# When the block sums run, and where a batch's last PSUM bank is copied, in a gated attention followed by a two-matrix feed-forward layer

## The chip, the cores and the metric

The kernel runs on one core of a Trainium2 chip. The core has a matrix engine (TensorE, PE in the profile), a vector engine (VectorE, DVE), a scalar engine (ScalarE, ACT), a general engine (GpSimd, POOL) and a queue that only issues transfers (SyncE, SP). Each runs its own instructions in the order in which they are written and waits for the others by semaphores. TensorE writes its results into PSUM, which is kept here as two pairs of banks and four single banks; everything else lies in SBUF. The metric is the device time of one execution in microseconds (us), the median of several runs.

## The reference, cut to what matters

```python
# u, v: (8, 3008, 256); z: (8, 3008, 64); w_in: (256, 2048); w_out: (2048, 256)
scores = (1 / S) * z @ z.transpose(0, 2, 1)          # S = 3008
attn   = maximum(scores, 0) ** 2
x      = (u * (attn @ v)).reshape(8 * 3008, 256)
h      = x @ w_in
out    = (h / (1 + exp(-1.702 * h))) @ w_out
```

## The kernel before

Each of the 8 batches is cut into 6 chunks of 512 tokens (the last is shorter). For a chunk, the scores against blocks of keys go into a pair of PSUM banks (`sc`), ACT applies Relu (`rl`), DVE squares it (`a`), and TensorE multiplies by V into two single banks (`o`); DVE multiplies those by u (`gate`, tile `xt`). The scores are symmetric, so many blocks are not computed again but transposed by transfers on the SP queue (`tt`, `ad`). `attend` (L324) gives a chunk as a list of steps; in the main loop (L792) a step n of chunk i comes after what is written out for it: transposes of u, loads, and `take` (L757), which issues the scores, the Relu and the square of one or two units ahead of their use. The table `SCHED` (L725) says at which steps `take` is called; for the first chunk of batches 1 to 6 that is once each at n = 5, 9, 13 and 17, twice at 24, and every third step from 30 on.

The feed-forward layer works on pairs of chunks, s = 0, 1, 2 (chunks 0 and 1, 2 and 3, 4 and 5). `up_group(b, q)` (L407) makes one of 48 groups of a batch, 16 for each pair: four matmuls into a bank pair (`hg`, two such pairs in all, shared with the scores), the gelu on ACT into one of two buffers `gf` (L435), and a scaling into half precision, `gt`, on DVE (L441), or on ACT for q % 8 in 1, 3, 5 from q = 16 on (L439). So a group's matmuls need the gelu of two groups before to be done, and a group's gelu needs the scaling of two groups before.

The second matrix product of a pair is done in seven products instead of eight, a scheme of Strassen's kind: the operands are block sums `S1` to `S4` of the `gt` tiles (`pair_sum`, L547, on DVE) and sums of the weights. A pair needs 16 sums. They are appended to a list `SUMS` when their `gt` tiles are written, and `some_sums(most)` (L458) issues one of them, or two where the list is longer than `most`. The products P1 to P7 (`pair_product`, L574) accumulate in three single banks; a finished bank is copied by ACT (L607, L609) or added by DVE (L611) into the output tile `y`, which is transposed and stored (`store`).

The first 16 groups of a batch, the head (q below `LAGY` = 16), run inside the attention steps of chunk 4 (of chunk 5 in the last batch). There are no products yet. The other groups follow after chunk 5, one group and one half product in turn (loop at L840). The products left over at the end run alone (L856), the drain; then `take(b + 1, 2)` issues the next batch's first two units, and what is left in the list `AFTER` is issued (L867). In batches 0 to 6 that is one instruction, the copy of the bank that P4 of the last pair leaves (L607). The order of all engines is the order of the program text; nothing is reordered.

Of the kernel before, what the change touches and what calls it, by code (L numbers as in the profile page):

```python
# [15 lines left out]
def kernel(  # L16
# [13 lines left out]
    AF = mybir.ActivationFunctionType  # L30
# [23 lines left out]
    FSC = csc * csc * float(S) * float(S)  # L54

    dve, act, pe, sp, pool = nc.vector, nc.scalar, nc.tensor, nc.sync, nc.gpsimd
# [263 lines left out]
    def full(b):  # L320

        return NCH - 2 if b < B - 1 else NCH - 1
# [74 lines left out]
    def blocks(b):  # L397

        return [(i, CH if i < NCH - 1 or b % 2 else LFULL) for i in range(NCH)]

    def paired(b, s):

        return b < B - 1 or s < NCH // 2 - 1
# [3 lines left out]
    def up_group(b, q):  # L407
        s, r = divmod(q, 2 * NFG)
        pair = paired(b, s)
        if pair:  # L410
            fg, e = (TILES if q >= 2 * NFG or b else TILES0)[r // 2], r % 2
            if fg >= NFG // 2:
                e = 1 - e
            k = 2 * s + e
        else:
            k, fg = divmod(q, NFG)
        i, n = blocks(b)[k]
        hg = ps2.tile([P, FFG, CH], F32, name="hg", tag="ps2")
        for e in range(FFG):
            ff = fg * FFG + e  # L420
            for c in range(NCC):
                pe.matmul(  # L422
                    hg[:, e, :n], W1[:, c, ff * P:(ff + 1) * P], XT[b, i][:, c, :n],
                    start=(c == 0), stop=(c == NCC - 1),
                )
        if pair:
            if r % 2 == 0:
                GT[b, s, fg, "pair"] = pa.tile([P, FFG, 2, CH], F16, name="gt", tag="tt", bufs=14)
            g = GT[b, s, fg, "pair"][:, :, k % 2, :n]
        else:  # L430
            if fg % 2 == 0:
                GT[b, k, fg // 2] = pa.tile([P, CB, CH], F16, name="gt", tag="tt", bufs=14)
            g = GT[b, k, fg // 2][:, (fg % 2) * FFG:(fg % 2 + 1) * FFG, :n]
        gf = pw.tile([P, FFG, CH], F32, name="gf", tag="gf")
        act.activation(gf[:, :, :n], hg[:, :, :n], AF.Gelu_apprx_sigmoid, scale=1.0 / FSC)  # L435
        if pair and q not in (LAGY - 7, LAGY - 6):
            some_sums()
        if q >= LAGY and q % 8 in (1, 3, 5):
            act.activation(g, gf[:, :, :n], AF.Copy, scale=FSC)  # L439
        else:  # L440
            dve.tensor_scalar(g, gf[:, :, :n], FSC, None, ALU.mult)  # L441
        if not pair:
            some_sums(8)
        if pair:
            some = (("S1", "S2", "S3"), ("S4",))[r % 2] if fg >= NFG // 2 else ()
            SUMS.extend([lambda m=m, fg=fg: pair_sum(b, s, fg - NFG // 2, m) for m in some])
            if r == 2 * NFG - 2 and s == NCH // 2 - 1:
                some_sums()
        elif fg in (NFG - 3, NFG - 1):
            SUMS.extend(left_sums(b, k, fg == NFG - 1))  # L450
# [7 lines left out]
    def some_sums(most=3):  # L458
        for s_ in [SUMS.pop(0) for _ in range(min(len(SUMS), 1 + (len(SUMS) > most)))]:
            s_()  # L460
# [37 lines left out]
    def left_sums(b, k, last):  # L498

        some = [("S1", 0), ("S2", 0)]  # L500
        if last:
            some = [("S1", 1), ("S2", 1)] + [(name, h) for name in ("S3", "S4") for h in range(2)]
        return [lambda m=m: left_sum(b, k, *m) for m in some]
# [70 lines left out]
    def pair_product(b, s, name, half):  # L574
        if name == "odd":
            odd_block(b, s)
            return
        w = blocks(b)[2 * s + 1][1]
        right = {
            "P1": W2K[:, LO, 0], "P2": W2K[:, HI, 0], "P3": W2K[:, HI, 1], "P4": WT[:, 3],  # L580
            "P5": WT[:, 0], "P6": WT[:, 1], "P7": WT[:, 2],
        }[name]
        raw = {"P1": "a11", "P2": "a12", "P4": "a22"}
        form = {"P3": "S4", "P5": "S1", "P6": "S2", "P7": "S3"}
        new = name in ("P1", "P2", "P5")
        if new and half == 0:
            ST[b, s, "bank" + name] = ps1.tile([P, CH], F32, name="st", tag="ps1")
        bank = ST[b, s, "bank" + {"P6": "P1", "P7": "P1", "P4": "P1", "P3": "P5"}.get(name, name)][:, :w]
        for ff in range(half * NFF // 4, (half + 1) * NFF // 4):
            m, f = divmod(ff, FFG)  # L590
            while name in form and (b, s, form[name], m) not in ST:
                SUMS.pop(0)()
            lhs = pair_part(b, s, raw[name])(m) if name in raw else ST[b, s, form[name], m]
            pe.matmul(  # L594
                bank, right[:, ff], lhs[:, f], start=new and ff == 0, stop=ff == NFF // 2 - 1, skip_group_check=True,
            )
        if half == 0:
            return
        for e, at in ((0, "P1"), (1, "P5")):
            if name == at:  # L600
                Y[b, 2 * s + e] = pw.tile([P, NCC, CH], F32, name="y", tag="y")
        copy = {"P1": (0, 0), "P5": (1, 1), "P6": (0, 1), "P4": (1, 0)}
        outs = {"P3": (0, 1), "P7": (1, 1), "P2": (0, 0)}
        e, c = copy.get(name) or outs[name]
        y = Y[b, 2 * s + e][:, c, :w]
        if name == "P4" and s == NCH // 2 - 1:
            AFTER.append([0, lambda: act.activation(y, bank, AF.Copy, scale=1.0 / FSC)])  # L607
        elif name in copy:
            act.activation(y, bank, AF.Copy, scale=1.0 / FSC)  # L609
        else:  # L610
            dve.scalar_tensor_tensor(y, bank, 1.0 / FSC, y, ALU.mult, ALU.add)  # L611
        last = s == NCH // 2 - 1
        if name == "P4" and last:
            LAST2.extend([lambda: store(b, 2 * s), lambda: store(b, 2 * s + 1)])
        elif name == "P2" and not last:
            store(b, 2 * s)
        elif name == "P4":
            AFTER.append([2, lambda: store(b, 2 * s + 1)])

    AFTER = []  # L620

    def product(b, k, name):
        mm = pairs(b, k)
# [87 lines left out]
    LAGY = 2 * NFG  # L711
# [49 lines left out]
    def fill(b):  # L761
        assert not queue
        queue.extend(u_ for i in range(NCH) for u_ in pieces(b, i))
# [28 lines left out]
    for b in range(B):  # L792
# [5 lines left out]
        for i in range(NCH):  # L798
            host = b + 1 if more and i == NCH - 1 else b
            if host > b:  # L800
                fill(host)
                LATE.append(host)
            for n, step in enumerate(attend(b, i, b == 0 and i == 0)):
                if b == 0 and i == 0 and n in (5, 24):
                    load_u(0, n // 24)
                if b == 0 and i == 0 and n == 2:
                    copies = first_zt(3)
                if b == 0 and i == 0 and n == 3:
                    copies()
                if b == 0 and i == 0 and n in FIRST_CAST:  # L810
                    first_cast(FIRST_CAST[n], True)
                if b == 0 and i == 0 and n in FIRST_ZT:
                    first_zt(FIRST_ZT[n])()
                if (i, n) in turn:
                    turn_u(b, turn[i, n])
                if (i, n) in ((3, 3), (3, 26) if more else (4, 14)) and LAST2:
                    LAST2.pop(0)()
                if (i, n) in load:
                    load_u(b, load[i, n])
                if b == 0 and (i, n) in CASTW:  # L820
                    cast_w(CASTW[i, n])
                if b == 0 and (i, n) in LOADW:
                    load_w(LOADW[i, n])
                if more and (i, n) == (NCH - 2, 2 if b else 16):
                    load_z(b + 1)
                if b == 0 and i == NCH - 1 and n in (8, 30, 42):
                    wsums.pop(0)()
                take(host, sched[i].get(n, 0))
                if i == full(b) and n >= HEAD and (n - HEAD) * LAGY // (2 * NJ - 10) >= head and head < LAGY:
                    up_group(b, head)  # L830
                    head += 1
                step()
# [7 lines left out]
        for q in range(head, nup):  # L840
# [7 lines left out]
            prods.pop(0)()  # L848
            for a_ in AFTER:
                a_[0] -= 1  # L850
            while AFTER and AFTER[0][0] < 0:
                AFTER.pop(0)[1]()
            if q >= 44 and late:
# [9 lines left out]
        if more:  # L863
            while late:
                late.pop(0)[1]()
            take(b + 1, 2)
            while AFTER:  # L867
                AFTER.pop(0)[1]()


# [28 lines left out]
```

## Time and profile before

| | |
|---|---|
| median of 3 runs | 1182.12 us (1180.68 to 1183.69) |
| profiled execution, its own time | 1179.04 us |
| its span, first to last instruction | 1177.2 us, granted TensorE clock 0.999 |
| PE busy | 1169.1 us, 99% |
| DVE busy | 870.7 us, 74% |
| ACT busy | 837.3 us, 71% |
| POOL busy | 212.4 us, 18% |
| copies at L607 | 7, of 0.50 or 0.60 us |

A row of the timeline gives the start in us from the span's start, the duration, the engine, the line of the kernel, the operation, the tiles (out<-in) with their shapes, and the number of like instructions that are merged in it; in brackets stands how long the engine was idle before it and what ended that. A row of the waits gives who waited for whom: us in total, how often, the longest. [...]

### The profile page before, as it was taken

To read this page: it belongs to the slowest core of one execution; us is meant where nothing else is said; L and a number is where in the kernel's file an instruction comes from. 1 tells how busy PE (TensorE), PEld (TensorE's weight loads), DVE (VectorE), ACT (ScalarE), POOL (GpSimd) and SP (SyncE) were. 2 spreads that over 40 slices of the span, in tenths; PEclk is the share of its full clock that TensorE was granted. 3 is DMA by queue.
4 is the path that set the end of the run, shared out by engine and by line. 5 is a ranking of instruction groups with operands and counts; after the bars stand their busy time and mean duration, and the time that the engine had idled before them with its cause. 6 is when DMAs were issued, how large, how long until landed. Compare 5 with 4: busy or idle time off the path is not lost.

```text
span 1177.2 us, 20867 instructions
## 1 busy us (share of the span) xinstructions
PE 1169.1 (99%) x7996; PEld 575.3 (49%) x7996; DVE 870.7 (74%) x1386; ACT 837.3 (71%) x941; POOL 212.4 (18%) x294
## 2 busy tenths in 40 slices
PE   9999999999999999999999999999999999999998
PEld 3544455444454445544455445554445544554446
DVE  7789866878658786587865877668876698664876
ACT  7878864688646886478864787647876478672785
POOL 3033101232012320132101321014200241001000
PEclk9999999999999999999999999999999999999999
DMA  9998399854998559975499755996559975697023
GB/s 224 207 130 124 73 171 163 98 94 85 174 154 101 91 99 175 154 94 87 99 171 151 102 89 110 173 158 91 90 98 176 142 108 83 115 172 140 1 36 72
DMA packets 459027, 143.47 MB, mean 122 GB/s; under 512 B 424624, under 2 KB 453040, under 8 KB 458928
## 3 DMA queue, kind: packets, MB, share of 16 engines
q1 hardware_dynamic: 402464, 102.36, 53.6%
q0 software_dynamic: 55104, 38.49, 22.1%
q8 instruction: 62, 1.02, 0.4%
q10 hardware_dynamic: 1360, 1.31, 0.4%
q14 instruction: 37, 0.30, 0.1%
HBM read 60.29 MB, written 24.64 MB: 72 GB/s over the span
## 4 chain that ended last, share of the span: by engine, by line
PE 96%; ACT 2%; DVE 1%; issue 0%; ACTq 0%; DVEq 0%
PE o L367 39%; PE hg L422 27%; PE st L594 23%; PE sc L235 6%; PE st L642 1%; ACT rl L256 1%; PE yp L568 1%; ACT gf L435 0%; DVE gt L441 0%; PE w L99 0%; DVE s L560 0%; ACT y L607 0%; ACT ZT L143 0%; DVE ut L202 0%; DVE s L558 0%
## 5 line engine op out<-in xcount | busy, mean ns | idle before, releaser
L435 ACT ACTIVATE gf<-hg 128x1024 f32<-128x1024 f32 (+1 forms) x384 | 383.1, 1001 | 124.0 <-PE hg L422 102.2
L256 ACT ACTIVATE rl<-sc 128x1024 f16<-128x1024 f32 (+1 forms) x301 | 288.2, 993 | 167.4 <-PE sc L235 123.2
L422 PE MATMUL hg<-xt,W 128*128 128x512 f16 (+1 forms) x1408 | 353.4, 374 | 1.6 <-ACT gf L435 1.6
L367 PEld LDWEIGHTS <-V 64*128 64x128 f16 (+1 forms) x4098 | 239.2, 94 | 231.3 <-issue 9.5
L367 PE MATMUL o<-a,V 64*128 64x512 f16 (+3 forms) x2278 | 298.1, 368 | 0.4 <-DVE a L270 0.4
L441 DVE TENSOR_SCALAR gt<-gf 128x1024 f16<-128x1024 f32 (+1 forms) x288 | 204.8, 712 | 107.3 <-ACT gf L435 105.0
L270 DVE TENSOR_TENSOR a<-rl 128x1024 f16<-128x1024 f16 (+1 forms) x266 | 178.1, 674 | 116.3 <-ACT rl L256 114.2
L195 POOL DMA_DIRECT2D uq<-in_u_dram x168 | 115.0, 694 | 727.3 <-PE sc L235 469.8
L422 PEld LDWEIGHTS <-W 128*128 128x128 f16 x1536 | 149.5, 98 | 178.8 <-issue 6.0
L367 PE MATMUL o<-tt,V 64*128 64x512 f16 (+1 forms) x1518 | 234.0, 377 | 0.0
L235 PE MATMUL sc<-ZT 64*128 64x512 f16 (+3 forms) x688 | 118.1, 356 | 0.9 <-ACT ZT L143 0.3
L594 PEld LDWEIGHTS <-WT 128*128 128x128 f16 x736 | 72.0, 98 | 79.7 <-issue 0.8
L439 ACT ACTIVATE gt<-gf 128x1024 f16<-128x1024 f32 (+1 forms) x96 | 98.1, 1021 | 3.1
L594 PE MATMUL st<-gt,W 128*128 128x512 f16 (+1 forms) x368 | 89.9, 370 | 0.0
L594 PE MATMUL st<-s,WT 128*128 128x512 f16 (+1 forms) x368 | 89.2, 370 | 0.0
L594 PE MATMUL st<-gt,WT 128*128 128x512 f16 (+1 forms) x368 | 88.7, 370 | 0.0
L594 PEld LDWEIGHTS <-W 128*128 128x128 f16 x552 | 53.8, 98 | 58.2
L384 DVE TENSOR_TENSOR xt<-o,ut 128x512 f16<-128x512 f32 x80 | 51.4, 684 | 27.9 <-PE o L367 27.9
L558 DVE TENSOR_TENSOR s<-s,gt 128x1024 f16<-128x1024 f16 (+1 forms) x92 | 62.3, 677 | 1.0
L556 DVE TENSOR_TENSOR s<-gt 128x1024 f16<-128x1024 f16 (+1 forms) x92 | 60.9, 662 | 2.1
L560 DVE TENSOR_TENSOR s<-gt,s 128x1024 f16<-128x1024 f16 (+1 forms) x92 | 60.9, 662 | 0.0
L235 PEld LDWEIGHTS <-ZT 64*128 64x128 f16 x688 | 39.7, 94 | 43.3 <-issue 8.6
(66 smaller groups left out, 686.3 us busy)
## 6 DMA issues: line engine op xcount, KB each, us to landing
out_dram<-yo SPq DMA_DIRECT2D x156, 128.0 KB, 2.8
uq<-in_u_dram POOLq DMA_DIRECT2D x140, 128.0 KB, 3.5
V<-in_v_dram POOLq DMA_DIRECT2D x35, 256.0 KB, 6.6
tt<-a SPq DMA_TRANSPOSE x232, 3.4
uq<-in_u_dram POOLq DMA_DIRECT2D x28, 112.0 KB, 5.0
out_dram<-yo SPq DMA_DIRECT2D x28, 96.0 KB, 6.6
uq<-in_u_dram SPq DMA_DIRECT2D x20, 128.0 KB, 4.1
wst<-in_moe_w_in_dram POOLq DMA_DIRECT2D x4, 512.0 KB, 5.9
```

Of the source, the lines that this page charges most:

```text
L195: eng.dma_start(uq[k * QW:(k + 1) * QW, :n // QW].rearrange("t q c k -> t q (c k)"), src[:, :, cs])
L235: pe.matmul(sc[:, r, :q1 - q0], zt[h, 2 * kp + r, :], zt[h].rearrange("d n p -> d (n p)")[:, q0:q1], start=True, stop=True,)
L256: act.activation(rl[:, :, :n], sc[:, :, :n], AF.Relu, scale=csc)
L270: dve.tensor_tensor(a[:, :, :n], rl[:, :, :n], rl[:, :, :n], ALU.mult)
L367: ins = pe.matmul(acc[c][:, :n], V16[b][h, j].rearrange("p (c k) -> p k c", k=NCC)[:, c], weights(b, i, j)[h], start=(k, m) == first[c], s ...
L422: pe.matmul(hg[:, e, :n], W1[:, c, ff * P:(ff + 1) * P], XT[b, i][:, c, :n], start=(c == 0), stop=(c == NCC - 1),)
L435: act.activation(gf[:, :, :n], hg[:, :, :n], AF.Gelu_apprx_sigmoid, scale=1.0 / FSC)
L439: act.activation(g, gf[:, :, :n], AF.Copy, scale=FSC)
L441: dve.tensor_scalar(g, gf[:, :, :n], FSC, None, ALU.mult)
L556: dve.tensor_tensor(s_, a21, a22, ALU.add)
L558: dve.tensor_tensor(s_, ST[b, s, "S1", m], a11, ALU.subtract)
L594: pe.matmul(bank, right[:, ff], lhs[:, f], start=new and ff == 0, stop=ff == NFF // 2 - 1, skip_group_check=True,)
```

## The change

There are two parts.

In a head (q < 16) `some_sums` is no longer called between a group's gelu and its scaling. It is called behind the scaling, in those groups where q % 4 is 0, 1 or 2, with the limit 8 instead of 3, so that it issues one sum a time. From q = 16 on, and in groups that are not paired, the order is as it was.

The copy of the last pair's P4 bank goes into a list of its own, `COPY`, and is issued in the next batch's first chunk ahead of step 22, instead of behind the drain's `take`. The loop that emptied `AFTER` at the end of a batch is gone.

```diff
@@ up_group
         act.activation(gf[:, :, :n], hg[:, :, :n], AF.Gelu_apprx_sigmoid, scale=1.0 / FSC)
-        if pair and q not in (LAGY - 7, LAGY - 6):
+        if pair and q >= LAGY:
             some_sums()
         if q >= LAGY and q % 8 in (1, 3, 5):
             act.activation(g, gf[:, :, :n], AF.Copy, scale=FSC)
         else:
             dve.tensor_scalar(g, gf[:, :, :n], FSC, None, ALU.mult)
-        if not pair:
+        if not pair or q < LAGY and q % 4 < 3:
             some_sums(8)
@@ pair_product
         if name == "P4" and s == NCH // 2 - 1:
-            AFTER.append([0, lambda: act.activation(y, bank, AF.Copy, scale=1.0 / FSC)])
+            COPY.append(lambda: act.activation(y, bank, AF.Copy, scale=1.0 / FSC))
...
-    AFTER = []
+    AFTER, COPY = [], []
@@ main loop
                 if (i, n) in ((3, 3), (3, 26) if more else (4, 14)) and LAST2:
                     LAST2.pop(0)()
+                if (i, n) == (0, 22) and COPY:
+                    COPY.pop(0)()
...
             take(b + 1, 2)
-            while AFTER:
-                AFTER.pop(0)[1]()
```

## The prediction

> **What bounds the kernel now.** I read the page's busy shares first, then TensorE's own waits, then the timeline around every place where a matmul starts late.
>
> ```profile
> PE 1169.1 (99%) x7996; PEld 575.3 (49%) x7996; DVE 870.7 (74%) x1386; ACT 837.3 (71%) x941; POOL 212.4 (18%) x294
> ```
> ```profile
> PE hg L422 <- ACT gf L435: 1.6, 2, 1.1
> ```
>
> TensorE is busy for 99% of the span; only stalls of TensorE are to be won. The list of waits understates them: four matmuls in a row last 1.03 us and each is recorded 0.38 long, so they start (1.03 - 0.38)/3 = 0.216 apart, and a matmul that starts up to 0.16 late leaves no idle row. So I compare starts. From the head of the first batch (q numbers the up groups of a batch):
>
> ```profile
> 78.46 0.59 PE L367 MATMUL o<-tt,V 128*128 128x512 f16 x2
> 79.52 1.02 PE L422 MATMUL hg<-xt,W 128*128 128x512 f16 x4 [0.47 <-ACT gf L435]
> 81.28 0.65 DVE L551 TENSOR_TENSOR gt<-gt 128x1024 f16<-128x1024 f16 x1
> 81.85 0.68 DVE L560 TENSOR_TENSOR s<-gt,s 128x1024 f16<-128x1024 f16 x1
> 82.44 1.31 DVE L441 TENSOR_SCALAR gt<-gf 128x1024 f16<-128x1024 f32 x1
> 83.85 1.02 ACT L435 ACTIVATE gf<-hg 128x1024 f32<-128x1024 f32 x1 [2.24 <-DVE gt L441]
> 84.93 1.02 PE L422 MATMUL hg<-xt,W 128*128 128x512 f16 x4 [1.14 <-ACT gf L435]
> ```
>
> Here two sums (81.28, 81.85) stand ahead of the scaling of q11 (82.44), its end frees gf for the gelu of q13 (83.85), and that frees the PSUM pair for the matmuls of q15 (84.93). Two attention matmuls before it started at 83.19 and 83.41, so q15 was due at 83.62: 1.31 late. Likewise q12 was due at 78.46 + 0.43 = 78.89 and came at 79.52 (0.63), and q11 was 0.14 late at 77.60. Sum 2.08 us. In later batches only q15 is late. Its due time is the start of q14 plus six matmuls, 1.30: 228.12 against 228.28, 374.39/374.50, 663.94/664.04, 953.35/953.46, and nothing in the batches at 517 and 807: 0.5 in all.
>
> The other place is a batch's first chunk:
>
> ```profile
> 308.42 0.60 ACT L607 ACTIVATE y<-st 128x512 f32<-128x512 f32 x1
> 308.90 1.04 ACT L256 ACTIVATE rl<-sc 128x1024 f16<-128x1024 f32 x1
> 310.00 0.39 PE L235 MATMUL sc<-ZT 64*128 64x512 f16 x2
> ```
>
> The last bank's copy (308.42) stands ahead of the Relu of step 5 (308.90 to 309.94), which frees the score pair that step 13 writes. Step 9's scores began at 308.77; with their 0.11 and four row-tile pairs at 0.216, step 13 was due at 309.74: 0.26 late. In batches of the other parity (163.72, copy 0.50) it is 0.15. Seven starts, 4 x 0.15 + 3 x 0.25 = 1.35.
>
> **The change, part by part.** *The copy (L606, L867, loop at L816).* It moves on ACT's queue alone, from behind the two drain Relus to step 22 of the next first chunk; no DMA and nothing on SP, POOL or DVE moves with it. With it gone, step 5's Relu starts at 308.42 and ends at 309.46; step 13 is due at 309.74, so its stall goes whole: -1.35. Next late would be step 17, which needs step 9's Relu (about 309.97 against 310.82): free. In its new place the copy takes 0.60 (0.50) of this row's idle:
>
> ```profile
> 313.20 6.39 ACT L256 ACTIVATE rl<-sc 128x896 f16<-128x896 f32 x7 [0.68 <-PE sc L235]
> ```
>
> Step 17's Relu ends at 312.53, the copy ends about 313.05, and the next Relu starts at 313.20: cost 0, by 0.15. That cover matters: the seven Relus behind it run back to back at 0.91 against scores every 0.865, and the last scores (318.79) follow the Relu that frees them (318.68) by 0.11. A copy later by d would cost up to 7 x (d - 0.25). The store of that block is issued in chunk 3, from about 344 on, over 30 us later. The bank is held some 4 us longer. Four banks serve these tiles; the other two product banks are emptied by 305.23 (three evacuations of 157.58 to 159.37 in the other parity) and chunk 0's first attention matmul starts at 306.61, so two free banks are there: 0. The upper bound, a chunk 0 that waited for the held bank, would be 306.6 to 312.5, 5.9 per batch; but those matmuls come before the Relus that the copy is queued behind, so the program could not run at all, and I exclude it.
>
> [...]
>
> *The sums in the head (L436, L442).* Same instructions, other order. Before, 13 of the 16 sums of the first pair ran in q0 to q15: two each at q11 and q12, none at q9 and q10, always ahead of the scaling. After, 9 run (8 in batch 0), one behind each scaling where q % 4 < 3. A sum occupies DVE for 0.60 (81.85 to 82.44 is 0.59), a scaling 0.60 (85.00 to 85.60). A pair is 1.20 and the groups come every 1.29 or 1.51, so DVE keeps up, and each fourth group has no sum.
>
> I walk batch 0 through by these rows, keeping POOL's copies where they are (0.6 added to whatever DVE runs, as in the 1.31 of 82.44). The scaling of q7 ends at 75.5 instead of 76.43, so q9's gelu starts at 75.7 and q11 is on time. q10's scaling, a sum and the 1.17 transpose (step 28) follow to 80.6; q11's scaling ends at 81.3 instead of 83.75, q13's gelu runs 81.35 to 82.37, and q15 is due at 82.85. The 2.08 goes whole, with 0.5 to spare. In batch 1, q11's scaling ends at 226.45 instead of 227.11, q13's gelu ends at 227.6 and q15 is due at 228.12; batches 2, 4 and 6 are alike: -0.5.
>
> *What comes back at q16.* Instead of 3 sums, 7 (8 in batch 0) are left, and from q16 on they run in twos ahead of the scalings as before. There DVE comes straight from the last gates:
>
> ```profile
> 102.18 0.68 DVE L558 TENSOR_TENSOR s<-s,gt 128x1024 f16<-128x1024 f16 x1
> 102.78 0.94 DVE L441 TENSOR_SCALAR gt<-gf 128x1024 f16<-128x1024 f32 x1
> ...
> 103.81 1.02 ACT L435 ACTIVATE gf<-hg 128x1024 f32<-128x1024 f32 x1 [0.88 <-DVE gt L441]
> ...
> 104.88 1.02 PE L422 MATMUL hg<-xt,W 128*128 128x512 f16 x4
> ```
>
> In batch 0 (above) the gelu of q18 ends at 104.83 and q20 starts at 104.88, on time, with nothing left. DVE cannot bring its lead from the head: at 98.64 it waits for a Relu (ended 98.59) and from there has 3.5 us of fixed work. One more sum ahead of q16's scaling makes q20 late by 0.6 less the 0.05: +0.55. Then 5 sums more than now run by q20, so q20's scaling comes at about 110.9 instead of 108.27, which is 110.3 on the delayed TensorE; q22's gelu starts at 111.0 instead of 110.63 and q24 is late by 0.37 less its slack of 0.1: +0.28. Together +0.83. Bounds: 0 if DVE gains its lead after all, 3.0 (five sums at 0.60) if nothing is hidden; I take 0.83 since it follows the rows next to it.
>
> In batches 1 to 6 the same gelu leaves room:
>
> ```profile
> 391.64 0.68 DVE L441 TENSOR_SCALAR gt<-gf 128x1024 f16<-128x1024 f32 x1
> ...
> 392.42 1.02 ACT L435 ACTIVATE gf<-hg 128x1024 f32<-128x1024 f32 x1
> ...
> 394.45 1.03 PE L422 MATMUL hg<-xt,W 128*128 128x512 f16 x4
> ```
>
> It ends at 393.44, 1.01 ahead of q20 (1.04 in batches 1, 3, 5); ACT's copy of q17 holds it to 392.42 anyway. Late by 0.5 it still hides. ACT is full there and carries that 0.5 on for some groups, under margins of 1.0 to 1.3. The products need the sums in time: the second half of P5 wants its S1 at about 395.75 and gets it at 394.2. In batch 7 q18's gelu waits for ACT. Cost 0.
>
> **The sum.** -1.35 - 2.08 - 0.5 + 0.83 = -3.1 us. The profiled execution took 1179.04 (span 1177.2 and 1.8 around it), so it would become 1175.9. It is 3.1 below the median of the runs; taken from that, 1182.12 - 3.1 = 1179.0.
>
> **Rivals.** *No payback*: batch 0's tail absorbs the sums; -3.93, 1178.2. For it: DVE sheds five sums (3.0) before q16. Against it: the 0.05 margin. *The order saves nothing in the head*: DVE is just as full, a sum behind one scaling delays the next, and q15 stays late; then only the copy counts, with the payback: -0.5, 1181.6. Against it: 4 to 5 sums fewer. For it: POOL's copies (81.94 to 83.21) slow whatever DVE runs. *Slower*: the backlog at q16 outruns the margin of 1.01 to 1.04 in all batches. It decides when the gelu of q18 is late by more than 1.03: each further 0.1 costs 0.7 over seven batches, so at 2.1 late (three and a half sums instead of the one counted) 7 x 1.07 eats the 3.93 and adds 3.5: 1185.7; at four sums, 2.4 late, 7 x 1.37 - 3.9 gives 1187.8. For it: the 0.94 scaling beside POOL's V loads. Against it: half the margin is left by my count.
>
> **How the numbers follow.** Likeliest 0.42, no payback 0.28, head saves nothing 0.15, slower 0.15. What a measurement can tell is about 0.3%, 3.5 us; the runs shown spread over 3.0. Faster by that means below 1178.6: I give it 0.45 of the likeliest and 0.75 of the no-payback case, 0.40. Slower (above 1185.7) has its case's 0.15, same the rest, 0.45. The range goes from no payback less half the runs' spread, 1176.5, past the third case to 1184.0, leaving out the slower case and little below.
>
> **What would show it.** In the changed profile: step 13's scores of each first chunk 0.97 after step 9's; an ACT copy in the gap before the run of seven Relus, which still starts 0.40 behind its scores; hg starts of the batch 0 head at 1.3 or 1.5 without the 0.63 and 1.31; DVE with sums behind scalings. The payback shows as q20 and q24 of batch 0 late. Wrong would be: hg q20 late in batches 1 to 6, an idle TensorE at 313 to 319, or an attention matmul waiting for a PSUM bank.

## The result, and the profile after

The changed kernel takes 1178.19 us (median; 1175.54 to 1181.57). The kernel before, run beside it on the same chip, took 1180.22 (1178.61 to 1183.69). The ratio is 0.9981 with a 95% interval of 0.9972 to 0.9990, so the change takes off 2.2 us, between 1.2 and 3.3. That is less than the 0.3% that the prediction named as the bound for telling a time from no change, though the interval excludes no change. The sum of -3.1 lies inside this interval, near its edge; the absolute 1179.0 was reckoned from a median of 1182.12, which the later runs of the kernel before put 1.9 lower.

The profiled execution took 1177.70 us (span 1175.9), against 1179.04 (1177.2). First the busy times and TensorE's longest waits, from the page and from the list of waits of the changed kernel:

```profile
PE 1167.6 (99%) x7996; PEld 552.7 (47%) x7996; DVE 874.3 (74%) x1386; ACT 837.8 (71%) x941; POOL 209.6 (18%) x294
```
```profile
PE hg L422 <- ACT rl L256: 1.7, 1, 1.7
PE w L99 <- DVE nil L75: 1.2, 1, 1.2
```

The wait for a gelu that headed this list before (1.6 in two places) is gone. In its place stands one wait of 1.7 that nobody forecast. As in the prediction, I count from starts: what every matmul's start comes later than its predecessor's streaming time (0.216 for one of 512 columns), summed over the execution, was some 13.0 us before and is 11.8 now, a difference like that of the spans.

**The copy's place.** The timeline of the changed kernel in the first chunk of batch 2:

```profile
308.81 0.27 PE L235 MATMUL sc<-ZT 64*128 64x256 f16 x2
309.79 0.38 PE L235 MATMUL sc<-ZT 64*128 64x512 f16 x2
312.21 0.59 ACT L607 ACTIVATE y<-st 128x512 f32<-128x512 f32 x1
312.59 0.54 PE L235 MATMUL sc<-ZT 64*128 64x448 f16 x4
312.99 6.39 ACT L256 ACTIVATE rl<-sc 128x896 f16<-128x896 f32 x7 [0.19 <-PE sc L235]
```

Step 13's scores (309.79) come 0.98 behind step 9's (308.81), where they came 0.26 late before. The copy (312.21 to 312.80) lies in the gap ahead of the run of seven Relus, which still starts 0.40 behind its scores. All seven stalls of 0.15 and 0.25 are gone, and no attention matmul and no product waits for one of the four single PSUM banks (the wait of 1.7 above is for a score pair in batch 0, and has another cause).

**The head of batch 0.** TensorE of the changed kernel at q13, q14 and q15:

```profile
81.72 1.03 PE L422 MATMUL hg<-xt,W 128*128 128x512 f16 x4
82.58 0.81 PE L367 MATMUL o<-tt,V 128*128 128x512 f16 x3
83.23 1.03 PE L422 MATMUL hg<-xt,W 128*128 128x512 f16 x4
84.09 0.59 PE L367 MATMUL o<-tt,V 128*128 128x512 f16 x2
84.53 1.03 PE L422 MATMUL hg<-xt,W 128*128 128x512 f16 x4
```

The groups come 1.51 and 1.30 apart, which is their streaming time. The three stalls of 0.14, 0.63 and 1.31 are gone.

**What took their place.** Three things. The first is a late load, on VectorE and TensorE:

```profile
60.99 1.25 DVE L202 STREAM_TRANSPOSE ut<-uq 128x1024 f32<-128x1024 f32 x1 [3.15 <-DMA uq<-in_u_dram]
...
63.81 1.02 PE L422 MATMUL hg<-xt,W 128*128 128x512 f16 x4 [1.72 <-ACT rl L256]
```

The transpose of u for chunk 3 waited 3.15 for its load and held up the squares queued behind it; the first up group came 1.89 late. In the profile before, the same transpose ran at 57.98 without a wait. This code is untouched by the change, and it runs ahead of everything that the change moves. The second is the first weight sum (L488, issued at step 8 of chunk 5 of batch 0), which now waits for the load of w_out:

```profile
91.57 1.23 DVE L488 TENSOR_TENSOR WT<-W 128x1024 f16<-128x1024 f16 x1 [1.24 <-DMA W<-in_moe_w_out_dram]
```

Before, it started at 91.47 straight behind VectorE's preceding work, with its second quarter of w_out landed at 90.95, only half a microsecond to spare. In the profile of before:

```profile
91.47 1.22 DVE L488 TENSOR_TENSOR WT<-W 128x1024 f16<-128x1024 f16 x1
```

The third is the payback behind q16, in other places than forecast:

```profile
102.56 1.02 ACT L435 ACTIVATE gf<-hg 128x1024 f32<-128x1024 f32 x1
...
103.45 0.69 DVE L441 TENSOR_SCALAR gt<-gf 128x1024 f16<-128x1024 f32 x1
...
105.25 0.68 DVE L556 TENSOR_TENSOR s<-gt 128x1024 f16<-128x1024 f16 x1
...
105.34 1.24 PE L594 MATMUL st<-s,WT 128*128 128x512 f16 x4
...
106.58 0.68 DVE L441 TENSOR_SCALAR gt<-gf 128x1024 f16<-128x1024 f32 x1
...
107.36 1.02 ACT L435 ACTIVATE gf<-hg 128x1024 f32<-128x1024 f32 x1 [1.02 <-DVE gt L441]
...
108.44 1.02 PE L422 MATMUL hg<-xt,W 128*128 128x512 f16 x4
```

P5's four matmuls at 105.34 last 1.24 instead of 1.03: its second half waits for S1 (105.25 to 105.93), 0.22. The matmuls of q22 (108.44) come 0.29 late, behind q20's gelu (107.36), which waited for q18's scaling (106.58). With 0.10 at q24 that is 0.61.

### The profile page after: what moved, and what is told of

It reads as the page before. It is cut to its first block, busy times and chain, and to the rows that moved or that the text cites. A ratio compares the mean times of both kernels' runs of the same rounds, so it can differ in the third digit from the quotient of the medians.

```text
span 1175.9 us, 20857 instructions
## 1 busy us (share of the span) xinstructions
PE 1167.6 (99%) x7996; PEld 552.7 (47%) x7996; DVE 874.3 (74%) x1386; ACT 837.8 (71%) x941; POOL 209.6 (18%) x294
## 3 DMA queue, kind: packets, MB, share of 16 engines
q8 instruction: 62, 1.02, 0.4%
q10 hardware_dynamic: 1360, 1.31, 0.4%
## 4 chain that ended last, share of the span: by engine, by line
PE 94%; DMA 2%; DVE 1%; issue 1%; ACT 1%; POOL 0%; SPq 0%; DVEq 0%; POOLq 0%; ACTq 0%
PE o L367 38%; PE hg L422 26%; PE st L594 22%; PE sc L235 5%; PE st L642 1%; DMA uq<-in_u_dram 1%; PE yp L568 1%; DMA W<-in_moe_w_out_dram 1%; ACT rl L256 0%; DVE a L270 0%; DMA zst<-in_z_dram 0%; PE w L99 0%; POOL zst L162 0%; POOL zst L158 0%; ACT ZT L143 0%
## 5 line engine op out<-in xcount | busy, mean ns | idle before, releaser
L367 PEld LDWEIGHTS <-V 64*128 64x128 f16 (+1 forms) x4098 | 219.7, 94 | 251.4 <-issue 9.4
L235 PE MATMUL sc<-ZT 64*128 64x512 f16 (+3 forms) x688 | 115.3, 356 | 0.8 <-ACT ZT L143 0.5
L202 DVE STREAM_TRANSPOSE ut<-uq 128x1024 f32<-128x1024 f32 (+1 forms) x48 | 58.3, 1215 | 3.2 <-DMA uq<-in_u_dram 3.2
L611 DVE SCALAR_TENSOR_TENSOR y<-st,y 128x512 f32<-128x512 f32 (+1 forms) x69 | 45.7, 663 | 19.9 <-PE st L594 19.1
```

What stands on the lines that cost most here:

```text
L235: pe.matmul(sc[:, r, :q1 - q0], zt[h, 2 * kp + r, :], zt[h].rearrange("d n p -> d (n p)")[:, q0:q1], start=True, stop=True,)
L367: ins = pe.matmul(acc[c][:, :n], V16[b][h, j].rearrange("p (c k) -> p k c", k=NCC)[:, c], weights(b, i, j)[h], start=(k, m) == first[c], s ...
```

## The experiments

The questions were which half of the change brings the 2.2 us, why the head's 2.08 does not arrive in full, and whether the small disputed steps (POOL's copy, the margin behind the moved bank copy) are what the prediction said. A time "against before" is always against the kernel before on the same chip; two variants are best compared by these ratios.

### Each half alone

e1 keeps the copy's new place and puts the sums back; e2 keeps the sums' new order and puts the copy back.

```diff
@@ e1, against the changed kernel
-        if pair and q >= LAGY:
+        if pair and q not in (LAGY - 7, LAGY - 6):
...
-        if not pair or q < LAGY and q % 4 < 3:
+        if not pair:
@@ e2, against the changed kernel
-            COPY.append(lambda: act.activation(y, bank, AF.Copy, scale=1.0 / FSC))
+            AFTER.append([0, lambda: act.activation(y, bank, AF.Copy, scale=1.0 / FSC)])
...
-                if (i, n) == (0, 22) and COPY:
-                    COPY.pop(0)()
...
+            while AFTER:
+                AFTER.pop(0)[1]()
```

> The copy is moved, the sums of the head stay ahead of the scalings. My theory: the seven late score matmuls at step 13 of each first chunk (0.15 or 0.25 us each) go and nothing else moves, so 1.35 us less than before; the three late starts of the first head (0.14, 0.63, 1.31) and the late q15 of batches 1, 2, 4 and 6 stay. Rival (the copy is only moved into another full stretch of ACT): 0 us, with late scores between steps 24 and 47.

> The sums of the head stand behind the scalings, the copy stays in the drain. My theory after both profiles: the 2.08 us of the first head go, 0.6 comes back between q19 and q24 of batch 0, q15 is on time in batches 2, 4, 6 (0.34 gained) and 0.17 to 0.18 late in batches 1, 3, 5 (0.36 lost against before): 1.5 us less than before. The rival from the prediction (the order saves nothing in the head): within 0.3 us of before. The step-13 lateness of the seven first chunks stays.

e1: 1178.26 us, ratio 0.9984 (0.9975 to 0.9993), 1.9 us less (0.8 to 2.9). Its trace shows none of the seven stalls. Of the head's it shows 0.40 and 1.32 (0.14, 0.63 and 1.31 before); of the late q15 in later batches only one, 0.12 in batch 2, though the sums stand where they stood before. Its timeline at q15 of batch 0:

```profile
84.63 1.02 PE L422 MATMUL hg<-xt,W 128*128 128x512 f16 x4 [1.16 <-ACT gf L435]
```

e2: 1180.22 us, ratio 1.0002 (0.9986 to 1.0018). The seven stalls are back and the head's are gone, yet nothing is gained, where 1.5 us was expected. Its VectorE timeline in the first steps of chunk 5 shows why:

```profile
88.17 0.42 DVE L247 TENSOR_TENSOR ad<-rl 128x512 f16<-128x512 f16 x1
91.65 1.23 DVE L488 TENSOR_TENSOR WT<-W 128x1024 f16<-128x1024 f16 x1 [3.06 <-DMA W<-in_moe_w_out_dram]
92.79 0.69 DVE L270 TENSOR_TENSOR a<-rl 128x1024 f16<-128x1024 f16 x1
```

VectorE comes to the first weight sum at 88.59 instead of 91.47, and w_out lands no earlier than before (91.56 against 90.95). VectorE stands idle for 3.06, the squares of the scores queue behind it, and four matmuls that wait for ACT's and VectorE's work on them start late between 94 and 100, by 0.56 + 0.52 + 0.14 + 0.55 = 1.77 us. (The 0.14 is at the first matmul of q16, which is some 0.1 late in the other profiles too, that of before among them, so the price is nearer 1.7.) This explains where most of the 2.08 can go, but one trace does not show that it is the rule. (In that execution another 1.13 was lost at 1079, at a transposed block that landed late; not a part of either kernel's difference.)

### Is the late load of u the spread?

The changed kernel's profile lost 1.89 us at the load of u for chunk 3. e3 (the kernel before) and e4 (the changed kernel) issue that load earlier.

```diff
-    LOAD0 = {(1, 14): 2, (2, 4): 3, (2, NJ + 20): 4, (4, 8): 5}
+    LOAD0 = {(1, 14): 2, (1, 40): 3, (2, NJ + 20): 4, (4, 8): 5}
```

> The kernel before, with the load of u for chunk 3 of batch 0 moved up from step 4 of chunk 2 to step 40 of chunk 1, two transposing transfers earlier in SP's queue. Theory: the spread of both kernels' times (about 5 us) comes from that load, which landed at 55.6 in the profile of before and at 60.97 in that of after, where it made the first up group 1.9 us late; earlier by some 3 us the load always lands in time, so the slowest of the runs go and the median falls by up to 1.5 us. Rival: the spread has another cause, and the times stay as spread as they are.

> The changed kernel with the same earlier load. If the load is what spreads the runs, the difference between this one and the one before it is the change's own worth, by the stalls in the two profiles 1.35 + 2.08 + 0.5 less 0.6 less 0.5, 2.8 us, and both spread less. Rival: no less spread, and a difference of 2 us as between the two kernels as they are.

e3: 1179.65 us (1178.34 to 1183.39), ratio 0.9998 (0.9987 to 1.0009). e4: 1177.77 (1175.64 to 1181.1), ratio 0.9985 (0.9974 to 0.9995). Neither the medians nor the spread moved; the rival was right, that load alone does not make the spread. The medians of the two differ by 1.9, not by the 2.8 expected. e4's profiled execution showed another late load in its stead, that of w_in's quarter for ACT's cast, and something I had not expected behind it. From its windows and its timeline:

```profile
core 0: us, PE busy (x) PEld busy (x) DVE busy (x) ACT busy (x) POOL busy (x), PEclk, DMA share, GB/s
72.00:76.00 4.00, 0.55 (x4) 0.25 (x3) 0.51 (x1) 2.50 (x3) 0.00 (x0) 1.00 1.64 137
76.00:79.00 3.00, 3.00 (x11) 1.11 (x10) 3.00 (x5) 1.63 (x3) 1.44 (x2) 0.63 1.20 136
```
```profile
73.50 1.06 ACT L482 ACTIVATE W<-wst 128x1024 f16<-128x1024 f32 x1 [3.61 <-DMA wst<-in_moe_w_in_dram]
75.51 1.02 PE L422 MATMUL hg<-xt,W 128*128 128x512 f16 x4 [3.45 <-ACT gf L435]
76.83 1.91 PE L422 MATMUL hg<-xt,W 128*128 128x512 f16 x4
```

The cast waits 3.61, TensorE stands for 3.45, and from 76.83 on eight matmuls start some 0.427 apart instead of 0.216 (four matmuls last 1.91 instead of 1.02), with a granted clock of 0.63 in that window. The stall cost 3.6 us at its place and 1.7 more behind it.

### The weight sums out of the way

If the gain of the head is lost at the weight sum that stands ahead of the squares, then taking that sum later must bring the gain out. e5 does this to the changed kernel, e6 to e1 (the copy's new place with the sums in the old order).

```diff
-                if b == 0 and i == NCH - 1 and n in (8, 30, 42):
+                if b == 0 and i == NCH - 1 and n in (30, 42):
                     wsums.pop(0)()
...
-            if b == 0 and q == head + 3:
+            if b == 0 and q in (head + 7, head + 11):
                 wsums.pop(0)()
```

> The changed kernel with the four weight sums of batch 0 moved: the first two from steps 8 and 30 of chunk 5... to steps 30 and 42, the last two from step 42 and q19 to q23 and q27. New theory: what the head of batch 0 gains is lost again at the first weight sum, which waits on DVE for the second quarter of w_out (landed at 91.5, DVE idle for 1.2 us in the changed kernel's profile and 3.1 us in that with the sums alone) and holds up the squares behind it; and at q19 to q24 (0.6 us), where the weight sums fill DVE. Without them there: no late scores in chunk 5, no late group at q20 to q24, 1 to 2 us less than the changed kernel, some 3 to 4 us less than before. Rival (the sums behind the scalings simply save nothing, whatever follows): as the changed kernel, 2 us less than before.

> The moved copy alone, with the same moved weight sums. By the new theory the weight sums stood in no one's way here (no wait at the first one, it ran at 91.2), so it is as the moved copy alone, 1.5 us less than before, and the difference to the run beside it is the worth of the sums' new order with its way clear: 2.0 us. By the rival both runs are alike.

e5: 1176.61 us, ratio 0.9972 (0.9961 to 0.9983). e6: 1178.5, ratio 0.9983 (0.9971 to 0.9995). e5's first weight sum has no wait, and no score of chunk 5 is late:

```profile
94.08 1.22 DVE L488 TENSOR_TENSOR WT<-W 128x1024 f16<-128x1024 f16 x1
```

One part of the expectation failed: q22 is 0.29 late in e5 as in the changed kernel, so the weight sum at q19 is not what makes it late; only the 0.10 at q24 is gone. In e6, where the head's stalls (0.40 and 1.38) stay, moving the weight sums brings nothing beyond e1. The medians of the two differ by 1.9 us, the ratios by 1.3; the intervals overlap, so it is the traces that carry the reading. (e5's profiled execution, 1180.74, is the slowest of its twelve: it lost 2.9 us at 1079.76, at a transposed block that landed late, and 1.7 more behind it, far from the weight sums.) The delay has a price that both show, here in e5's timeline:

```profile
112.09 1.22 DVE L490 TENSOR_TENSOR WT<-W 128x1024 f16<-128x1024 f16 x1
...
113.36 0.82 PE L594 MATMUL st<-gt,WT 128*128 128x512 f16 x3 [0.47 <-DVE WT L490]
```

The third weight sum is now too late for P7: 0.63 late in e5, 0.59 in e6.

### How much room the moved copy has, and the sum beside POOL's copy

e7 puts the bank's copy at step 30, in the middle of the seven Relus. e8 leaves q10 of every head without a sum, since in the changed kernel the sum there runs beside POOL's copy of z.

```diff
@@ e7, against the changed kernel
-                if (i, n) == (0, 22) and COPY:
+                if (i, n) == (0, 30) and COPY:
@@ e8, against the changed kernel
-        if not pair or q < LAGY and q % 4 < 3:
+        if not pair or q < LAGY and q % 4 < 3 and q != 10:
```

> The changed kernel with the copy at step 30 instead of 22, between the second and third of the Relus that run back to back. By the prediction's reading of that stretch (each Relu 0.91 after the last, scores every 0.865, margins of 0.27, 0.22, 0.17 and 0.11 at the last four scores) 0.5 us more on ACT makes the scores of steps 39 to 45 late, about 0.4 us in each of seven batches: 2.8 us more than the changed kernel. Rival (ACT has room there): as the changed kernel.

> The changed kernel without the sum behind q10's scaling. There POOL's copy (223.47 to 224.75 in batch 1) stretches the sum to 1.31, and with the transpose behind it q11's scaling ends at 227.16, so q15 is 0.17 late in batches 1, 3 and 5. Theory: without that sum q11's scaling ends 0.6 to 1.2 earlier and q15 is on time in all batches. Rival: POOL's copy stretches the transpose or the scaling instead, and q15 stays late by 0.1 or more.

e7: 1179.6 us, ratio 0.9999 (0.9984 to 1.0015): the gain is lost, as expected, some 1.4 us against the changed kernel by the medians and 2.1 by the ratios, with intervals that overlap; both are less than the 2.8 of stalls expected. ACT's timeline:

```profile
312.89 0.60 ACT L607 ACTIVATE y<-st 128x512 f32<-128x512 f32 x1
313.37 4.71 ACT L256 ACTIVATE rl<-sc 128x1024 f16<-128x1024 f32 x5
```

In batch 2 the scores behind the copy start 0.17 late and the next three 0.036 late each, 0.28 in all: TensorE goes at ACT's pace from there. In the odd batches, where the copy takes 0.50, it is 0.07 and three times 0.037, 0.18. The seven batches make 3 x 0.28 + 4 x 0.18 = 1.6, which lies between the 1.4 and the 2.1 in the times; the 0.4 per batch that was expected is nearly twice the 0.22 measured. (The profiled execution lost another 1.28 at 442.41, where a block sum stood behind a transposition that had waited 1.37 for the transfer of an earlier output block; it lies outside the stretch where the copy stands.)

e8: one profiled execution of 1177.64 us. In the changed kernel's first profile, batches 1, 3 and 5 had q15 0.17 to 0.18 late. Batch 1 in the timeline of that profile:

```profile
223.47 1.28 POOL L162 COPY zst<-zst 128x768 f16<-128x768 f16 x1 [4.77 <-DMA zst<-in_z_dram]
...
223.98 1.31 DVE L558 TENSOR_TENSOR s<-s,gt 128x1024 f16<-128x1024 f16 x1
...
225.21 1.23 DVE L202 STREAM_TRANSPOSE ut<-uq 128x1024 f32<-128x1024 f32 x1
...
226.37 1.52 DVE L441 TENSOR_SCALAR gt<-gf 128x1024 f16<-128x1024 f32 x2
...
227.25 1.94 ACT L435 ACTIVATE gf<-hg 128x1024 f32<-128x1024 f32 x2 [1.11 <-DVE gt L441]
...
228.32 1.02 PE L422 MATMUL hg<-xt,W 128*128 128x512 f16 x4
```

The sum behind q10 (223.98) lasts 1.31 instead of 0.69 beside POOL's copy (223.47 to 224.75). The transpose and q11's scaling follow it, the gelu of q13 starts at 227.25, and q15 comes at 228.32. In e8 no head is late, but P5 waits 0.81 for its S1 in batch 0, since the sum left out of the head is missed there, and the w_out wait shows again, 3.21 at L488, with 0.71 + 0.53 + 0.14 + 0.55 in chunk 5 and at q16 and q17. Whether a head is late also changes from one execution to another: e7, and e9 and e10 below, with the sum at q10, have no late q15 either (e11 one of 0.06). So e8's time and trace do not show that the sum at q10 is the cause; the rows above do, for batch 1 of that execution.

In the changed kernel's first profile six block sums began while a copy of POOL's ran (83.53, 215.78, 223.98, 361.79, 513.02 and 650.83). Each took 1.31 and ended 0.54 or 0.55 behind the copy, little less than the 0.60 that a sum occupies VectorE by itself; the one above ends at 225.29, the copy at 224.75. In batch 3 it is again the sum behind q10 (513.02). In batch 5 that sum (802.84) took 0.68; there q9's scaling (800.16) took 1.35, beside a copy from 800.13 to 800.96. Not everything that VectorE runs beside such a copy takes longer: in the profile of before a transpose (223.94, beside a copy from 223.46 to 224.71) took 1.24, where the full ones of that line (L202) without such a copy took 1.23 to 1.24. The 0.6 that the prediction adds to whatever VectorE runs is thus its estimate from one row (82.44). No run here shows what makes the others longer.

### The sums alone again, and a better place for the weight sums

e9 is e2 with the weight sums of e5. e10 is the changed kernel with the weight sums at steps 30 and 42 of chunk 5 and at q = 19 and 27, so that the third is early enough for P7.

```diff
@@ e10, against e5
-            if b == 0 and q in (head + 7, head + 11):
+            if b == 0 and q in (head + 3, head + 11):
```

> Against the kernel before: the block sums are moved as in the change, the bank copy stays where it was, and the weight sums of batch 0 are taken at steps 30 and 42 of chunk 5 and at q = 23 and 27 instead of at steps 8, 30, 42 and q = 19. Theory (moving the sums is worth some 2 us, and the change alone loses part of that because the first weight sum stands in DVE's queue waiting for w_out): no late scores in chunk 5 of batch 0, step 13 of the first chunks late as before (1.35 in all), 2.0 to 2.6 us of head stalls gone, 0.6 lost at the third weight sum near 112 us and 0.4 to 0.6 at the groups behind q = 16, so about 1.3 us less than before, ratio 0.9989. Rival (the sums' order is worth nothing and the earlier run without the moved weight sums showed that): ratio 1.000 or above.

> The changed kernel, with the weight sums of batch 0 at steps 30 and 42 of chunk 5 and at q = 19 and 27. Theory: the first has its quarter of w_out when it is issued (no wait there), the third is ready before P7 wants it near 112 us, so that the stall of 0.63 seen with q = 23 goes; the sum at q = 19 costs the groups behind it what it costs in the changed kernel, 0.3 to 0.6. About 0.3 to 0.4 us less than the version with q = 23 and 27, 3.3 to 3.7 less than before, ratio 0.997. Rival (the 0.63 only moves, to P5 or to the groups q = 22 to 24, since DVE has no room before 112): the same time as the version with q = 23 and 27, with a new stall of about 0.6 between 104 and 112.

e9: 1178.87 us, ratio 0.9988 (0.9977 to 1.0000), the 0.9989 of the theory. Its trace has no late score in chunk 5, no head stall, the seven copy stalls, and 0.63 at P7. (In that execution the load of u was late, 2.32 at the first up group.) Against e2 (1.0002) only the weight sums' places differ. That interval ends at no change, so by the times alone the sums' worth is likely but not certain; with the stalls that go from one trace to the other it stands.

e10: 1176.26 us, ratio 0.9965 (0.9951 to 0.9978), 4.1 us less than before (2.6 to 5.8); 3.3 to 3.7 was expected. Its timeline:

```profile
94.01 1.22 DVE L488 TENSOR_TENSOR WT<-W 128x1024 f16<-128x1024 f16 x1
...
112.76 1.03 PE L594 MATMUL st<-gt,WT 128*128 128x512 f16 x4
```

The first weight sum has no wait, and P7 (112.76) is on time. What is left behind q16 is 0.13 at P5, 0.29 at q22 and 0.10 at q24, and the excess over streaming is some 9.4 us, against 13.0 before: 3.6 less. It beats the kernel before beyond its interval; against the changed kernel the interval overlaps (0.9972 to 0.9990).

### The changed kernel once more

> The changed kernel as it is, profiled once more. In its first profiled execution the load of u for chunk 3 came late (1.89 us at 61.7), so that all that follows came 1.9 us later and the first weight sum waited for w_out only 1.2 us. Theory: where that load is on time, the first weight sum waits about 3 us and chunk 5 of batch 0 shows late starts of 0.6, 0.5, 0.1 and 0.6, some 1.8 in all, which eat most of the 2.08 that the head gained; the time is the same 1178 or so by another road. Rival: the stalls in chunk 5 belong to the two kernels in which they were seen (without the copy's move, without the sum behind q10) and do not show here; then this execution takes about 1176.

This execution took 1181.56 us, slower than the one of before beside it (1180.98), and one trace holds both losses. From its timeline:

```profile
62.05 1.25 DVE L202 STREAM_TRANSPOSE ut<-uq 128x1024 f32<-128x1024 f32 x1 [3.89 <-DMA uq<-in_u_dram]
...
64.87 1.65 PE L422 MATMUL hg<-xt,W 128*128 128x512 f16 x4 [2.47 <-ACT rl L256]
...
95.93 1.23 DVE L488 TENSOR_TENSOR WT<-W 128x1024 f16<-128x1024 f16 x1 [2.86 <-DMA W<-in_moe_w_out_dram]
...
98.92 0.37 PE L235 MATMUL sc<-ZT 64*128 64x448 f16 x2 [0.19 <-ACT rl L256]
...
100.41 0.39 PE L235 MATMUL sc<-ZT 64*128 64x512 f16 x2 [0.37 <-ACT rl L256]
...
103.55 1.02 PE L422 MATMUL hg<-xt,W 128*128 128x512 f16 x4 [0.39 <-ACT rl L256]
```

The u load was late again (2.63 at the first up group, and 1.6 more behind it, as in e4). And the first weight sum waited 2.86, with starts late by 0.36 + 0.53 + 0.14 + 0.55 = 1.58 us in chunk 5 and just behind it. So the chunk-5 stalls do belong to the changed kernel: the rival falls. The expectation had a part wrong: a late u load does not cover the w_out wait, since here both came.

## Why the prediction was right, and where it was not

**The copy (-1.35): right.** All seven stalls went and the new place cost nothing, with the 0.98 and the 0.40 that the working gave. e1 measured -1.9 (-2.9 to -0.8) for it alone. That no matmul waits for the held bank is shown too: holding the bank some 4 us longer (the copy starts at 312.21 instead of 308.42) cost nothing here.

**The head of batch 0 (-2.08): the stalls went, the gain did not stay.** This is the step that failed. The working stopped at q15 being on time, and asked what is late next only behind q16. Between them lie the weight sums. TensorE 2.08 earlier, and VectorE with its sums of the head spread out, bring VectorE to L488 some 2.9 earlier (88.59 in e2 against 91.47), while its quarter of w_out lands at 91.56. Its margin before, 0.5 us between landing and use (0.1 in e1, 1.9 in e3), could be read from the trace of before, and the prediction has no term for it. The price depends on when w_out lands. A wait of 2.86 to 3.21 costs 1.5 to 1.8 us in chunk 5 and just behind it, without the 0.1 that is there in any case (e2, e8, e11), so that of the 2.08 only 0.3 to 0.6 is kept; one of 1.24 or 1.18 (the first profile of the changed kernel, e7), or none (e4), costs nothing that the starts show. Where that sum stands later (e5, e9, e10), no such stall is left. The 2.08 is itself one profile's: the others with the sums in the old order show 1.72 (e1), 1.79 (e3) and 1.78 (e6).

**q15 in later batches (-0.5): not kept in the first profile.** The stalls of before are gone in batches 2, 4, 6, but the sum behind q10 (batches 1 and 3) or q9's scaling (batch 5) fell beside POOL's copy of z in the first profile, took 1.31 or 1.35, and those batches are late by 0.17 to 0.18. That is 0.52, as much as before; it is 0.33 in e5 and none in e7, e9 and e10. Nor is the 0.5 there in every execution of the old order: e1, e3 and e6 show 0.1 to 0.3. So this term is not a fixed one. What the working missed is the end of q11's scaling, put at 226.45 in batch 1: it left POOL's copy out there, after adding it in batch 0. The scaling ended at 227.16.

**The payback (+0.83): right in size, wrong in place.** It measured 0.61. It was forecast at q20 (0.55) and q24 (0.28), by way of q18's gelu waiting for q16's scaling as before. That gelu (102.56) did not wait for that scaling (103.45 to 104.14): it began where ACT's own copy of q17 ended, so it wrote the buffer which that copy had freed. Which buffer a gelu gets had changed with the order. The sums' delay came out at P5's second half instead, which was worked out for batches 1 to 6 only, and at q22. In batches 1 to 7 nothing is late behind q16: right.

**The total.** The terms as measured are -1.35 - 2.08 + 0.61 = -2.8, with between 0 (the first profile) and -0.5 for q15: -2.8 to -3.3. With chunk 5's price added, 0 to 1.8 us from one execution to another, that is -3.3 to -1.0; measured was -2.2 (-3.3 to -1.2). The two profiled executions differ by 1.34, but there the u load alone cost 1.89. That the forecast of 1179.0 came so close is luck: two errors went against each other. The base, the median of 1182.12, was 1.9 too high, and the gain taken off it about 0.9 too large. (By its own reckoning the lower end of the range is 1178.2 - 1.5 = 1176.7, not 1176.5; nothing hangs on it.)

**The rivals.** No payback is refuted by 0.61 us of stalls; that its time, 1178.2, is the one measured is chance. The order saves nothing in the head is refuted in the head, and yet the changed kernel is about as fast as the copy alone (0.9981 against 0.9984), through a wait that this rival did not name. Slower is refuted: the backlog never outran the margins of batches 1 to 6.

What stays open is how often the changed kernel meets the w_out wait in full: of the six profiles with the sums' new order and the weight sum in its old place, three show it at about 3 us (one of them with a late u load), two at 1.2 and one not at all. Issuing w_out's load earlier, instead of using it later, was not tried.

## What to carry to other kernels

When stalls are removed, everything behind them comes earlier, and each load that was in time by less than that can become the next wait: read the margin of every DMA-fed instruction downstream, here 0.5 us at the first weight sum, before a gain is booked. An instruction that waits for a load should not stand in an engine's queue ahead of work that TensorE needs (in e2 VectorE stood idle for 3.06 at L488, and TensorE's starts were late by 1.77); put it where the load has landed and check the consumer on the other side (P7, 0.63 late in e5). A late instruction that fills a gap (the copy) is worth its stalls and no more, 1.35 here, and it is safe only as far as the gap reaches: at step 30 it made 1.6 of new ones (e7).

## What the runs showed of the hardware that I had not expected

In three executions a stall of TensorE cost more than its length. After 2.47 us without a matmul (e11), eight starts from 65.08 on were about twice as far apart as before. Its windows, with the columns of e4's above:

```profile
62.00:65.00 3.00, 0.53 (x3) 0.19 (x2) 2.94 (x5) 1.10 (x2) 0.35 (x1) 1.00 1.07 241
65.00:68.00 3.00, 3.00 (x8) 1.01 (x7) 2.39 (x6) 2.50 (x3) 0.00 (x0) 0.52 1.14 203
```

The granted clock is 0.52 from 65 to 68, against 1.00 from 62 to 65, and 1.6 us went with it. The same followed idle times of 2.73 (e5, ending at 1079.76; clock 0.51 in the 3 us from 1080) and 3.45 (e4, clock 0.63 in the window above), and did not follow 2.16 (e9) and 1.72 (the changed kernel's first profile), where the clock stayed at 1.00. In the whole-span clock this hardly shows (0.998 in e11). No run here varied the idle time alone, and none shows why one idle time was followed by it and another was not.

The other surprise is the spread of the loads in the first 100 us: the same transpose of u found its load landed in some executions and waited 3.15 and 3.89 in others, with no change in the code that issues it. A single profile cannot tell such a loss from the effect of a change; the late starts have to be put to their lines first.
